# Second pass: the first layer's second product as seven half-size block products, its weights cut by output half

## The chip, the cores and the metric

One core of a Trainium2 chip runs the whole program. TensorE (PE in the profile; PEld is its loading of the stationary operand) does the matmuls, VectorE (DVE) and ScalarE (ACT) the element work, and SyncE (SP) issues nearly all DMAs, in its program's order. The metric is device microseconds of one execution; the median of the runs counts.

## The reference, cut to what matters

```python
x = softmax(30 * tanh(q @ k.T / 8 / 30)) @ v     # 4 batches, 12 heads, 448 positions, head size 64
x = x.transpose(0, 2, 1, 3).reshape(1792, 768)
h = x @ w_in                                     # first layer: 768 -> 2048
x = (h - np.tanh(h)) @ w_out                     # 2048 -> 768
h = x @ w_in2                                    # second layer
out = (h / (1 + np.exp(-1.702 * h))) @ w_out2
```

All weights arrive as 64-bit floats. The rows that count here are the two products with a 2048 x 768 matrix, above all `(h - tanh(h)) @ w_out`.

## The kernel before, in words

**Precision.** Each operand of the four large products is kept as two fp32r tiles, a rounded part and what is left (`xh`/`xl`, `gh`/`gl`, `wh`/`wl`). A product takes three matmuls for each block: high by high, low by high, high by low.

**Stages.** `attention` comes first, in 24 pair steps `g`. Then the 1792 rows go through both layers in two passes of 896 rows (two batches of 448). Each pass runs `gemm_in(0)` (first layer, first product, L648), `gemm_out` (first layer, second product, L667), `gemm_in(1)` (L648 again) and a last product by rows: `gemm_out_rows` (L690) in the first pass, `gemm_rows_seven` (L743, L728) in the second. The 896 columns of `x` and `g` are streamed as 512 and 384 (`SPANS`); the weights are the stationary operand except in the last product.

**Weights.** They come in chunks of the list `chunks`, used in the order of `stream`. In the first pass each chunk is loaded as 64-bit (`dbl_dma`, tile `wd`), converted by six steps on ScalarE and VectorE (`conv_exp` to `conv_lo`, tiles `wr`, `wh`, `wl`), and its two halves are stored to DRAM (`kept`). In the second pass they are loaded back: `w_next` takes the next chunk, `ahead` calls `prepare(i + LEAD)` with `LEAD` 2, so loads run two chunks ahead; the pool `whl` holds three chunks. `gemm_out` uses 18 chunks: six output blocks by three parts of the 2048.

**The last product of the second pass** uses seven block products of half size in place of eight (Strassen-Winograd form). Its weights need sums of blocks, `t1` to `t4`. `weight_combos` makes them: for each of four quarters `j` it loads eight halves (`load_sum`), adds and subtracts on VectorE, splits on ScalarE and VectorE (`keep_split`), and stores eight halves. It is a generator; each call of `ahead` advances it one step (`side`). The left sums of `g` are made beside the matmuls by `left`, into the tiles `ring`.

**What sets the order.** The attention part and `gemm_in` are pinned to the order written. Elsewhere a list scheduler places the instructions of each engine, so the order of the built program is not that of the code: in the built kernel before, most of `weight_combos` stands beside `gemm_in(0)` of the second pass. An engine runs its own list strictly in order, SP too: a DMA that waits for its source holds back all DMAs behind it.

**Early work.** In `attention`, `early` names nine chunks that are loaded and converted there; `conv_at` and `split_at` are tables that say in which pair step. `load_qk`, `load_v` issue the inputs of a step.

Of the kernel before, what the change touches and what calls it, by code (L numbers as in the profile page):

```python
# [29 lines left out]
LATE_AT = 8  # L30
# [7 lines left out]
def attention_moe_moe(ctx, tc, q, k, v, cap, w_in1, w_out1, w_in2, w_out2, out):  # L38
# [82 lines left out]
    parts = [(0, 6), (6, 11), (11, 16)]  # L121
    WG = 3
    chunks = []
    for layer, (wi, wo) in enumerate(((w_in1, w_out1), (w_in2, w_out2))):
        wi, wo = wi.bitcast(U32), wo.bitcast(U32)
        for f in range(KF):
            chunks.append((wi[:, 2 * f * P:2 * (f + 1) * P], 0, KM, P))
        if layer == 0:
            for e in range(KM):
                for f0, f1 in parts:  # L130
                    chunks.append((wo[:, 2 * e * P:2 * (e + 1) * P], f0, f1, P))
        else:
            for half in range(2):
                for f in range(0, KF, 2):
                    chunks.append((wo[:, 2 * half * HW:2 * (half + 1) * HW], f, f + 2, HW))
# [50 lines left out]
    def conv_lo(i):  # L186
        h, l = whl[i]
        n = width[i]
        lo_dve(l[:, :n], raws.pop(i)[:, :n], h[:, :n])
# [5 lines left out]
    def convert(i):  # L195
# [7 lines left out]

    R0 = NCH - KF
    KQ = KF // 4
    combos = {m: [dr_p.tile([P, 2, WC], F32, name=f"{m}_{j}") for j in range(KQ)] for m in ("t1", "t2", "t3", "t4")}
    block = {
        "b11": kept[R0:R0 + KQ],
        "b21": kept[R0 + KQ:R0 + 2 * KQ],
        "b12": kept[R0 + 2 * KQ:R0 + 3 * KQ],  # L210
        "b22": kept[R0 + 3 * KQ:],
        **combos,
    }
    PRODUCTS = ("b11", "t2", "b21", "t3", "t1", "t4", "b22")
    stream = [(kept[i], width[i], chunks[i][3]) for i in range(NCH)] * (NPASS - 1)
    stream += [(kept[i], width[i], chunks[i][3]) for i in range(R0)]
    stream += [(t, WC, HW) for m in PRODUCTS for t in block[m]]

# [45 lines left out]
    def weight_combos():  # L264
        for j in range(KQ):
# [4 lines left out]
            r11, r12, r21, r22 = slots  # L270
            for dst, m in zip(slots, ("b11", "b12", "b21", "b22")):
                load_sum(dst, block[m][j])
                if m != "b22":
                    yield
            t1 = wr_p.tile([P, WC], F32, tag="wr", name="t1")
            hi = wr_p.tile([P, WC], F32, tag="wr", name="t1h")
            nc.vector.tensor_tensor(out=t1, in0=r12, in1=r11, op=ALU.subtract)
            nc.vector.tensor_tensor(out=r12, in0=r22, in1=r12, op=ALU.subtract)
            nc.vector.tensor_tensor(out=r11, in0=r12, in1=r11, op=ALU.add)
# [604 lines left out]
```

## Time and profile before

| | us |
|---|---|
| median of 3 runs (1141.86 to 1146.07) | 1145.31 |
| profiled execution | 1144.08 |
| its span | 1142.3 |

| stage of the profiled execution | from, to (us) |
|---|---|
| attention | 0 to 214 |
| first pass: L648, L667, L648, L690 | 214 to 334, to 450, to 567, to 683 |
| second pass: L648, L667, L648, L743 with L728 | 683 to 799, to 916, to 1032, to 1138 |

TensorE is busy in 1130.9 of 1142.3 us, VectorE in 705.3, ScalarE in 632.1. A busy TensorE row counts pipelined matmuls, whose records overlap, so the time that a matmul adds is read from the spacing, that is from a stretch divided by its count, and not from the mean duration of one. The same holds for back-to-back instructions of VectorE, whose records overlap by some 0.1 us.

### The profile page before, as it was taken

To read this page: it belongs to the slowest core of one execution; us is meant where nothing else is said; L and a number is where in the kernel's file an instruction comes from. 1 tells how busy PE (TensorE), PEld (TensorE's weight loads), DVE (VectorE), ACT (ScalarE), POOL (GpSimd) and SP (SyncE) were. 2 spreads that over 40 slices of the span, in tenths; PEclk is the share of its full clock that TensorE was granted. 3 is DMA by queue.
4 is the path that set the end of the run, shared out by engine and by line. 5 is a ranking of instruction groups with operands and counts; after the bars stand their busy time and mean duration, and the time that the engine had idled before them with its cause. 6 is when DMAs were issued, how large, how long until landed. Compare 5 with 4: busy or idle time off the path is not lost.

```text
span 1142.3 us, 15746 instructions
## 1 busy us (share of the span) xinstructions
PE 1130.9 (99%) x5699; PEld 930.3 (81%) x5699; DVE 705.3 (62%) x1096; ACT 632.1 (55%) x923; POOL 1.8 (0%) x16
## 2 busy tenths in 40 slices
PE   9999999999999999999999999999999999999998
PEld 3443433588888989888999998888898888889998
DVE  4698998699996445777754557999500022445441
ACT  6889998799995444666644427888200022213230
POOL 0000000000000000000000000000000000000000
PEclk9999999999999999999999999999999999999999
DMA  6476776455447666666687888677833333338784
GB/s 162 102 200 187 201 209 190 163 195 192 157 141 267 237 226 218 220 221 221 229 255 256 281 287 307 208 270 268 284 103 106 120 111 111 111 111 282 227 265 153
DMA packets 165022, 230.00 MB, mean 201 GB/s; under 512 B 59680, under 2 KB 112464, under 8 KB 164944
## 3 DMA queue, kind: packets, MB, share of 16 engines
q1 hardware_dynamic: 162496, 227.84, 61.9%
q10 hardware_dynamic: 2448, 1.15, 0.4%
q8 instruction: 45, 0.74, 0.3%
q14 instruction: 33, 0.27, 0.1%
HBM read 157.68 MB, written 71.26 MB: 200 GB/s over the span
## 4 chain that ended last, share of the span: by engine, by line
PE 96%; DMA 3%; DVE 1%; SPq 0%; ACT 0%; issue 0%; DVEq 0%
PE ps_h L648 41%; PE ps_y L667 20%; PE ps_o L690 10%; PE ps_o L743 7%; PE ps_sc L362 5%; PE ps_pv L395 5%; PE ps_sc L358 1%; PE ps_o L728 1%; PE ps_pv L392 1%; PE ps_r L404 1%; PE ps_qk L338 1%; PE ps_qk L347 1%; DMA wd<-in_moe_w_in_dram 1%; DMA wh<-t 0%; DMA raw<-in_k_dram 0%; DMA wl<-t 0%
## 5 line engine op out<-in xcount | busy, mean ns | idle before, releaser
L648 PE MATMUL ps_h<-xh,wh 128*128 128x384 f32 (+1 forms) x768 | 279.2, 364 | 1.7 <-DMA wh<-kept 1.7
L648 PE MATMUL ps_h<-xl,wh 128*128 128x512 f32 (+1 forms) x768 | 280.5, 365 | 0.0
L648 PE MATMUL ps_h<-xh,wl 128*128 128x512 f32 (+1 forms) x768 | 174.7, 362 | 0.0
L648 PEld LDWEIGHTS ps_h<-xh,wh 128*128 128x128 f32 x768 | 144.1, 188 | 18.6 <-DMA wh<-kept 2.4
L648 PEld LDWEIGHTS ps_h<-xl,wh 128*128 128x128 f32 x768 | 144.2, 188 | 16.4
L648 PEld LDWEIGHTS ps_h<-xh,wl 128*128 128x128 f32 x768 | 139.5, 188 | 16.3 <-issue 1.4
L667 PE MATMUL ps_y<-gl,wh 128*128 128x384 f32 (+1 forms) x384 | 140.4, 366 | 0.0
L667 PE MATMUL ps_y<-gh,wh 128*128 128x384 f32 (+1 forms) x384 | 139.7, 364 | 0.0
L667 PE MATMUL ps_y<-gh,wl 128*128 128x384 f32 (+1 forms) x384 | 88.4, 362 | 0.0
L588 ACT ACTIVATE g_t<-ps_h 128x512 f32<-128x512 f32 x64 | 34.9, 546 | 91.4 <-PE ps_h L648 90.6
L82 DVE TENSOR_TENSOR wl<-wr,wh 128x768 fp32r<-128x768 f32 (+1 forms) x66 | 61.4, 931 | 36.7 <-PE ps_y L667 18.9
L160 ACT ACTIVATE wr<-wd 128x768 f32<-128x768 f32 (+1 forms) x66 | 57.8, 877 | 47.0 <-DVE wl L82 32.5
L177 DVE SCALAR_TENSOR_TENSOR wr<-wd,wr 128x768 uint32<-128x768 uint32 (+1 forms) x66 | 61.6, 933 | 30.5 <-ACT wd L165 29.4
L76 ACT CAST wh<-wr 128x768 fp32r<-128x768 f32 (+1 forms) x66 | 53.6, 812 | 46.2 <-PE ps_y L667 29.9
L667 PEld LDWEIGHTS ps_y<-gl,wh 128*128 128x128 f32 x384 | 72.1, 188 | 8.3
L667 PEld LDWEIGHTS ps_y<-gh,wh 128*128 128x128 f32 x384 | 72.0, 188 | 8.1
L667 PEld LDWEIGHTS ps_y<-gh,wl 128*128 128x128 f32 x384 | 69.8, 188 | 7.6
L690 PE MATMUL ps_o<-wh,gh 128*128 128x384 f32 x224 | 74.8, 334 | 0.0
L690 PE MATMUL ps_o<-wl,gh 128*128 128x384 f32 x224 | 74.8, 334 | 0.0
L690 PE MATMUL ps_o<-wh,gl 128*128 128x384 f32 x224 | 74.8, 334 | 0.0
L374 ACT ACTIVATE t<-ps_sc,tsc 128x896 f32<-128x896 f32 x72 | 69.8, 1003 | 6.8 <-PE ps_sc L362 5.9
L82 DVE TENSOR_TENSOR xl<-ps_y,xh 128x512 fp32r<-128x512 f32 (+1 forms) x24 | 14.9, 621 | 93.2 <-ACT xh L76 93.2
(120 smaller groups left out, 1841.1 us busy)
## 6 DMA issues: line engine op xcount, KB each, us to landing
wd<-in_moe_w_in_dram SPq DMA_DIRECT2D x64, 384.0 KB, 4.2
wh<-kept SPq DMA_DIRECT2D x59, 384.0 KB, 3.2
wl<-kept SPq DMA_DIRECT2D x59, 384.0 KB, 4.6
kept<-wh SPq DMA_DIRECT2D x54, 384.0 KB, 3.4
kept<-wl SPq DMA_DIRECT2D x54, 384.0 KB, 3.8
wd<-in_moe_w_out_dram SPq DMA_DIRECT2D x16, 768.0 KB, 5.6
wd<-in_moe_w_out_dram SPq DMA_DIRECT2D x24, 384.0 KB, 4.0
pair<-kept SPq DMA_DIRECT2D x16, 384.0 KB, 6.1
```

The source lines that it names most:

```text
L76: pin(nc.scalar.copy(out=dst, in_=src))
L82: pin(nc.vector.tensor_tensor(out=dst, in0=src, in1=hi.bitcast(F32), op=ALU.subtract))
L160: pin(nc.scalar.mul(out=raws[i][:, :width[i]], in_=dbls[i][:, :, 1].bitcast(F32), mul=2.0 ** -112))
L177: pin(nc.vector.scalar_tensor_tensor(out=u, in0=dbls.pop(i)[:, :, 1], scalar=0x80000007, in1=u, op0=ALU.bitwise_and, op1=ALU.bitwise_or))
L362: pin(nc.tensor.matmul(ps[:, j, :S], qk[a, kc], qk[a, :S], start=True, stop=True))
L374: pin(nc.scalar.activation(out=t, in_=ps, func=AF.Tanh, scale=tsc))
L395: pin(nc.tensor.matmul(ps[j * D:(j + 1) * D, :S], rawv[g][:, j, c, :], tt[g, c][:, j], start=(c == 0), stop=(c == KC - 1)))
L588: nc.scalar.activation(out=t, in_=ps, func=AF.Tanh, scale=0.5 * GELU_C)
L648: pin(nc.tensor.matmul(ps, w[:, kk, :], x[kk][:, a], start=(m == 0), stop=(m == len(seq) - 1)))
L667: nc.tensor.matmul(p[:, :a1 - a0], w[:, f - f0, :], x[f][:, a0:a1], start=(c == 0 and m == 0), stop=(c == len(parts) - 1 and m == len(seq) ...
L690: nc.tensor.matmul(ps[n][:, :HW], g[2 * j + ff][:, a], w[:, ff, :], start=(j == 0 and m == 0), stop=(j == KF // 2 - 1 and m == len(seq) - 1),)
L743: nc.tensor.matmul(ps[n], x[:, t], w[:, kk, :], start=(k == 0 and m == 0), stop=(k == KH - 1 and m == 2),)
```

## The change

1. **Chunks.** The first layer's `w_out` is cut as the second layer's already is: by output half (384 columns) and two blocks of the 2048, 16 chunks of one size in place of 18.
2. **First pass.** `gemm_out` runs over output halves, with six PSUM banks (three output blocks by two spans) open at a time; its results are split by `x_out`.
3. **Second pass.** `gemm_out_seven` takes the place of `gemm_out`: seven products `SEVEN_A`, each 8 blocks of the 2048 by 3 output blocks by 3 matmuls of 448 columns. `right` makes the sums of `g` on VectorE and splits them into `ring`. The partial products are kept in `part` tiles and added on VectorE. So `gemm_in(0)` of this pass leaves `g` unsplit (`gr`).
4. **Weight sums.** `weight_combos(0)` makes `s1` to `s4` from a new single-precision copy (`single`, stored in the first pass by `conv_lo`) beside `gemm_in(0)`; `weight_combos(1)`, that of before, comes one stage later, beside `gemm_out_seven` and `gemm_in(1)`.
5. **Early steps.** The first `load_qk(1)` issues its query half from SP, not from ScalarE; the two first 64-bit loads are issued in steps 1 and 3, not both in step 0; one conversion moves from step 21 to 20, and two splits change places.

```diff
-        if layer == 0:
-            for e in range(KM):
-                for f0, f1 in parts:
-                    chunks.append((wo[:, 2 * e * P:2 * (e + 1) * P], f0, f1, P))
...
+        if A0 <= i < A0 + KF:
+            nc.sync.dma_start(out=single[i - A0], in_=raw_w)
+        if A0 + 2 * KQ <= i < A0 + 3 * KQ:
+            return
...
+    SEVEN_A = ("11", "s2", "12", "s3", "s1", "22", "s4")
...
+                if layer == 0:
+                    nc.sync.dma_start(out=r[m], in_=single[n * KQ + j])
+                else:
+                    load_sum(r[m], block[1][m][j])
...
-    conv_at = [3, 5, 7, 9, 11, 13, 15, 17, 21]
-    split_at = [10, 11, 12, 15, 16, 20, 17, 18, 19, 21, 21, 22]
+    conv_at = [3, 5, 7, 9, 11, 13, 15, 17, 20]
+    split_at = [10, 11, 12, 15, 16, 19, 17, 18, 20, 21, 21, 22]
...
-        load_qk(1, nc.scalar)
+        load_qk(1)
...
-            if g == 0:
-                dbl_dma()
+            if g in (1, 3):
                 dbl_dma()
...
+    def right(p, k):
+        g11, g12, g21, g22 = (gr[f][:, t * S:(t + 1) * S] for f in (k, KH + k) for t in range(2))
+        if p == 1:
+            x = s2[k]
+            nc.vector.tensor_tensor(out=x, in0=g22, in1=g12, op=ALU.subtract)
+            nc.vector.tensor_tensor(out=x, in0=x, in1=g11, op=ALU.add)
+        elif p == 3:
...
+        split(ring[k], x)
...
+    def gemm_out_seven():
...
+        for p, name in enumerate(SEVEN_A):
+            ps = three()
+            for j in range(KQ):
+                i, (wh, wl) = w_next()
+                ahead(i)
+                for kk in range(2):
+                    k = 2 * j + kk
+                    h, l = (t[:, :S] for t in ring[k])
+                    for e in range(3):
+                        c = slice(e * P, (e + 1) * P)
+                        for m, (w, x) in enumerate(((wh, h), (wh, l), (wl, h))):
+                            nc.tensor.matmul(
+                                ps[e], w[:, kk, c], x, start=(k == 0 and m == 0), stop=(k == KH - 1 and m == 2)
+                            )
+                    if p < 6:
+                        right(p + 1, k)
...
+                x_out(3 * m_ + e, slice(s_ * S, (s_ + 1) * S), x)
...
-        yield from gemm_in(0)
-        if last:
-            side.append(weight_combos())
-        gemm_out()
         if last:
             plain[0] = True
             open_plain()
+            side.append(weight_combos(0))
+        yield from gemm_in(0)
+        if last:
+            for _ in side.pop():
+                pass
+            side.append(weight_combos(1))
+        (gemm_out_seven if last else gemm_out)()
         yield from gemm_in(1)
```

Three places of the built order carry terms of the prediction. The first is SP in the second pass, while the first layer's second product runs; a row is one DMA of 128 x 768 words, `wh`/`wl` are weight loads, `pair`/`lo` are loads and `t` stores of `weight_combos`. In the kernel before:

```order
L232 DMA wh_7655<-kept23_196 128x640
L232 DMA wl_7656<-kept23_196 128x640
L232 DMA wh_7699<-kept24_197 128x640
L232 DMA wl_7700<-kept24_197 128x640
L232 DMA wh_7744<-kept25_198 128x768
L232 DMA wl_7745<-kept25_198 128x768
```

In the changed kernel, around the loads of the last product's weights (`s4`):

```order
L257 DMA pair_8178<-kept62_235 128x768
L258 DMA lo_8291<-kept62_235 128x768
L235 DMA wh_8317<-s4_0_261 128x768
L235 DMA wl_8318<-s4_0_261 128x768
L235 DMA wh_8349<-s4_1_262 128x768
L235 DMA wl_8350<-s4_1_262 128x768
L265 DMA t1_2_243<-hi_8322 128x768
L265 DMA t1_2_243<-first_8321 128x768
L235 DMA wh_8391<-s4_2_263 128x768
L235 DMA wl_8392<-s4_2_263 128x768
L265 DMA t3_2_259<-pair_8178 128x768 x2
L235 DMA wh_8417<-s4_3_264 128x768
```

Weight loads that stood alone now have loads and stores of the weight sums between them, and the load of `s4_2` stands behind a store of `first_8321`.

The second place is VectorE at the end of that stage. Before, the last output block's low parts and then the first gate of the next product (`gr`):

```order
L82 TENSOR_TENSOR xl4_124<-ps_y_7958,xh4_118 128x512
L82 TENSOR_TENSOR xl4_124<-ps_y_7959,xh4_118 128x384
L82 TENSOR_TENSOR xl5_125<-ps_y_8085,xh5_119 128x512
L82 TENSOR_TENSOR xl5_125<-ps_y_8086,xh5_119 128x384
L591 SCALAR_TENSOR_TENSOR gr0_8218<-g_t_8317,ps_h_8290 128x512
```

After, from the end of the sixth product (bank `ps_y_8254`):

```order
L729 TENSOR_TENSOR part_7687<-ps_y_8254,part_7687 128x448
L259 TENSOR_TENSOR pair_8178<-pair_8178,lo_8291 128x768
L82 TENSOR_TENSOR xl3_123<-part_7687,xh3_117 128x448
L286 TENSOR_TENSOR pair_8178<-pair_8178 128x768
L263 TENSOR_TENSOR first_8321<-first_8321,hi_8322 128x768
```

and at the end of the seventh:

```order
L729 TENSOR_TENSOR part_7819<-ps_y_8388,part_7819 128x448
L729 TENSOR_TENSOR part_7820<-ps_y_8389,part_7820 128x448
L729 TENSOR_TENSOR part_7821<-ps_y_8390,part_7821 128x448
L82 TENSOR_TENSOR xl0_120<-part_7819,xh0_114 128x448
L82 TENSOR_TENSOR xl1_121<-part_7820,xh1_115 128x448
L82 TENSOR_TENSOR xl2_122<-part_7821,xh2_116 128x448
```

The additions of the weight sums and of the partial products now stand in VectorE's list ahead of what SP and TensorE wait for; the next product starts with `xh0`, `xl0`.

The third place is SP at the end of attention, where the first reload of chunk 0 is issued (`wh<-kept0`). Before:

```order
L413 DMA xd3_3_107<-xs_1967 128x448
L151 DMA wd_1997<-in_moe_w_in_dram 128x3x256 x2
L413 DMA xd3_4_108<-xs_2016 128x448
L232 DMA wh_2049<-kept0_173 128x768
L191 DMA kept14_187<-wh_2025 128x768
```

After:

```order
L446 DMA wb_1985<-wrow1_111 64x448 x2
L145 DMA wd_1966<-in_moe_w_in_dram 128x3x256 x2
L427 DMA xd3_3_107<-xs_2002 128x448
L235 DMA wh_2079<-kept0_173 128x768
L190 DMA kept14_187<-wh_2011 128x768
```

The reload now stands behind the store of step 21's result (`xd3_3`) and no longer behind that of step 22 (`xd3_4`).

## Rows read from the trace of the kernel before

**Rows 1.** The page's part 1: busy us, share of the span, instructions.
```profile
PE 1130.9 (99%) x5699; PEld 930.3 (81%) x5699; DVE 705.3 (62%) x1096; ACT 632.1 (55%) x923; POOL 1.8 (0%) x16
```

**Rows 2.** The chain of waits, second pass's L667 stage: start, us, what.
```profile
799.27 116.40 PE ps_y L667 x576
```

**Rows 3.** Stretches by engine: both L667 stages and the last product.
```profile
core 0: us, PE busy (x) PEld busy (x) DVE busy (x) ACT busy (x) POOL busy (x), PEclk, DMA share, GB/s
799.20:915.60 116.40, 116.40 (x578) 104.42 (x577) 22.15 (x33) 12.56 (x21) 0.00 (x0) 1.00 0.47 151
1031.80:1138.40 106.60, 105.29 (x601) 103.62 (x599) 43.33 (x83) 27.12 (x54) 0.00 (x0) 1.00 0.75 242
333.60:450.10 116.50, 116.50 (x578) 104.52 (x577) 65.05 (x95) 58.83 (x72) 0.00 (x0) 1.00 0.66 227
```

**Rows 4.** The same chain in the two last products by rows (384-column matmuls).
```profile
567.92 115.09 PE ps_o L690 x664
...
1048.58 14.04 PE ps_o L743 x81
...
1080.91 4.65 DMA wl<-t
...
1105.66 5.00 DMA wh<-t
```

**Rows 5.** The chain in attention: eight matmuls of 448 columns.
```profile
36.21 1.70 PE ps_sc L362 x8
```

**Rows 6.** VectorE in order of time, back to back: start, us, instruction.
```profile
200.69 0.62 DVE L79 COPY xs<-ps_pv 128x448 f32<-128x448 f32 x1
201.24 0.62 DVE L474 TENSOR_TENSOR xs<-xs,wb 128x448 f32<-128x448 f32 x1
...
202.36 0.96 DVE L177 SCALAR_TENSOR_TENSOR wr<-wd,wr 128x768 uint32<-128x768 uint32 x1
203.23 0.62 DVE L82 TENSOR_TENSOR xl<-xs,xh 128x448 fp32r<-128x448 f32 x1
```

**Rows 7.** Groups by shape, busy us and mean ns: the cast of 448 columns.
```profile
L76 ACT CAST xh<-x 128x448 fp32r<-128x448 f32 x12 | 6.8, 568 | 23.1 <-DVE x L810 23.1
```

**Rows 8.** DMA issues, reloads of weights: KB each, us to landing.
```profile
wh<-kept SPq DMA_DIRECT2D x59, 384.0 KB, 3.2
wl<-kept SPq DMA_DIRECT2D x59, 384.0 KB, 4.6
```

**Rows 9.** Stretches in which the DMA engines were busiest (second pass's first product).
```profile
690.00:697.00 7.00, 7.00 (x36) 6.25 (x35) 5.83 (x11) 5.48 (x11) 0.00 (x0) 1.00 1.01 375
...
686.00:700.00 14.00, 14.00 (x71) 12.59 (x71) 10.29 (x17) 10.48 (x19) 0.00 (x0) 1.00 0.90 296
...
690.00:704.00 14.00, 14.00 (x71) 12.51 (x70) 12.28 (x21) 11.50 (x22) 0.00 (x0) 1.00 0.96 345
```

**Rows 10.** TensorE in order of time: attention's step 1, and its end.
```profile
25.20 1.72 PE L395 MATMUL ps_pv<-t,rv 128*64 128x448 f32 x8
...
214.29 0.50 PE L648 MATMUL ps_h<-xh,wh 128*128 128x512 f32 x1 [1.67 <-DMA wh<-kept]
```

**Rows 11.** The chain of waits in attention: start, us, what.
```profile
10.98 2.39 DMA raw<-in_k_dram
...
21.64 7.17 DMA wd<-in_moe_w_in_dram
...
34.55 1.65 PE ps_pv L395 x8
...
43.00 1.65 PE ps_pv L395 x8
...
209.75 4.50 DMA wh<-kept
```

**Rows 12.** SP's own issue of two input loads near the start.
```profile
8.34 1.27 SPq L302 DMA_DIRECT2D raw<-in_q_dram  x2
```

**Rows 13.** A stretch in `gemm_in(0)` of the second pass.
```profile
774.00:781.00 7.00, 7.00 (x37) 6.30 (x36) 7.00 (x13) 5.55 (x11) 0.00 (x0) 1.00 0.48 159
```

More of the change, by code (lines that the diff above doesn't have):

```diff
@@ L127, in attention_moe_moe @@
             chunks.append((wi[:, 2 * f * P:2 * (f + 1) * P], 0, KM, P))
-        if layer == 0:
-            for e in range(KM):
-                for f0, f1 in parts:
-                    chunks.append((wo[:, 2 * e * P:2 * (e + 1) * P], f0, f1, P))
[L132 to L135, printed above, removed]
+        for half in range(2):
+            for f in range(0, KF, 2):
+                chunks.append((wo[:, 2 * half * HW:2 * (half + 1) * HW], f, f + 2, HW))
     NCH = len(chunks)
@@ L262, in keep_split, with weight_combos @@
             nc.sync.dma_start(out=dst[:, m], in_=t)
-    def weight_combos():
+    def weight_combos(layer):
+        names = (("11", "12", "21", "22"), ("11", "21", "12", "22"))[layer]
         for j in range(KQ):
@@ new lines, in weight_combos, with op @@
+            first_ = wr_p.tile([P, WC], F32, tag="wr", name="first")
+            hi = wr_p.tile([P, WC], F32, tag="wr", name="hi")
+            def op(out, a, kind, b):
+                nc.vector.tensor_tensor(out=out, in0=a, in1=b, op=kind)
+            if layer == 0:
+                op(first_, r["21"], ALU.add, r["22"])
+                op(r["21"], r["11"], ALU.subtract, r["21"])
+                op(r["11"], first_, ALU.subtract, r["11"])
+                op(r["12"], r["12"], ALU.subtract, r["11"])
+                made = (("s1", first_, hi), ("s3", r["21"], r["22"]), ("s2", r["11"], None), ("s4", r["12"], None))
+            else:
+                op(first_, r["12"], ALU.subtract, r["11"])
+                op(r["12"], r["22"], ALU.subtract, r["12"])
+                op(r["11"], r["12"], ALU.add, r["11"])
+                op(r["21"], r["21"], ALU.subtract, r["11"])
+                made = (("t1", first_, hi), ("t3", r["12"], r["22"]), ("t2", r["11"], None), ("t4", r["21"], None))
@@ L288, in weight_combos @@
+            yield
+            for m, x, h in made:
+                keep_split(block[layer][m][j], x, h or wr_p.tile([P, WC], F32, tag="wr", name="hi"))
                 yield
@@ L572, in rest @@
             nc.vector.copy_predicated(out=q, mask=m.bitcast(U16), data=far)
-            splits.append(g_split(a, f, q))
+            if not plain[0]:
+                splits.append(g_split(a, f, q))
             for _ in last:
                 pass
+            if plain[0] and f < KH and a.stop == NT:
+                right(0, f)
         def rest_behind():
@@ L581, in g_cubic @@
         late.append(rest_behind)
-        if f == KF - 1 and a.stop == NT:
+        if f == KF - 1 and a.stop == NT and not plain[0]:
             late.append(lambda: list(splits.pop(0)))
@@ L636, in left @@
             x = {0: g11, 2: g12, 5: g22}[p]
-        split(ring[k], x)
+        split([t[:, :TH] for t in ring[k]], x)
     def gemm_in(layer):
@@ L673, in gemm_out @@
                             ahead(i)
-                        if m == LATE_AT:
+                        if a0 == 0 and e == 1:
                             run_late()
-            for (a0, a1), p in zip(SPANS, ps):
-                hi_act(xh[e][:, a0:a1], p[:, :a1 - a0])
-                lo_dve(xl[e][:, a0:a1], p[:, :a1 - a0], xh[e][:, a0:a1])
+                    if j == KF // 2 - 1:
+                        for e in range(3):
+                            x_out(3 * half + e, slice(a0, a1), bank[e][:, :a1 - a0])
@@ L821, in moe @@
             open_plain()
+            side.append(weight_combos(0))
[5 more added lines that the diff above has]
+        (gemm_out_seven if last else gemm_out)()
         yield from gemm_in(1)
+        if last:
+            for _ in side.pop():
+                pass
         (gemm_rows_seven if last else gemm_out_rows)(b0)
```

155 lines of the change are left out of this document (100 added, 55 removed).

## The prediction

> **What bounds the kernel now.** The page's first part says TensorE: busy in 1130.9 of 1142.3 us [rows 1]. That alone is weak, since its records overlap, so the next view is the chain of waits stage by stage. In the second pass's first-layer second product the chain is one piece, 576 matmuls in 116.40 us with nothing between them [rows 2]: 0.2021 us each, at a mean of 448 columns (512 and 384 in equal number). No other engine matters there: VectorE is busy 22.15 of 116.40 us and DMA moves 151 GB/s [rows 3]. So a matmul taken out is time taken out, as long as nothing else becomes late. The last product shows where such a form hurts: its matmuls cost 14.04/81 = 0.1733 us, the 588 of them (504 of L743, 84 of L728) are 101.9 us, and the stage takes 106.6 [rows 3, 4], so 4.7 us go into waits, the two longest pieces of them for weight loads.
>
> **The change part by part.** I sum against the profiled execution, 1144.1 us (span 1142.3 and 1.8 outside it).
>
> *Matmuls.* Seven products of 8 x 3 x 3 are 504 matmuls of 448 columns for 576 of the same mean width: 72 less. This form is not in the trace at 448 columns. From below it costs 0.1733 us (384 columns [rows 4]); from above 0.213, eight attention matmuls of 448 columns in 1.70 us [rows 5]. I take 0.2021, since that mixes a narrower and a wider matmul of the same type and the price is in proportion to columns. 504 x 0.2021 = 101.9 us, **-14.5 us**. At 0.213 the gain is 9.0, and 0.1733 would make it 29.1, which I give no weight.
>
> *VectorE in the new stage.* The built order has 141 instructions there: 106 of 448 columns, 32 of 768, 3 of 384. Back to back they follow each other at 0.55 and 0.87 us [rows 6], so 58 + 28 + 1.5 = 88 us beside 102 of TensorE. Each product's sums are made while the product before runs, a lead of up to 14.55 us (72 x 0.2021), so I cost this at nothing. With the recorded durations of 0.62 and 0.96 as prices it is 98 us: still under, but the cover is thin (a rival below).
>
> *The end of the stage.* Before, the next product started without a gap [rows 2]. Now its first matmuls need `xh0`, `xl0`, which come from the seventh product. Bank 0 is ready 6 matmuls early, 1.2 us. Then VectorE adds (0.62), ScalarE casts (0.57 [rows 7]), and `xl0` stands behind the two other additions (the second place above): the last bank's addition starts about 0.2 us after the last matmul and holds VectorE 0.55, then `xl0` takes 0.62 [rows 6]: 1.4 us after the end, when 0.2 would have done. **+1.2 us**, between 1 and 2.5.
>
> *DMA in the new stage.* A weight half is 384 KB [rows 8], 393 KB in thousands. At the best rate of the trace, 375 GB/s with the DMA engines fully busy [rows 9], it takes 1.05 us. In SP's list from the third to the seventh product there are 76 such transfers: 40 weight halves and 36 of `weight_combos(1)`, which used to lie beside the first product and now meets 28 chunks of weights where there were 18 smaller ones. 76 x 1.05 = 79.7 us of transfer for 5 x 14.55 = 72.8 of TensorE: 6.9 too much. A load is issued two chunks ahead, 2 x 18 x 0.2021 = 7.28 us, and lands 3.2 to 4.6 us later [rows 8], so some 3.3 us can be late unseen. **+3.6 us.** The lower bound is 0, if the first two products run ahead enough. The upper one takes the best stretch of 14 us that I found, 345 GB/s [rows 9]: 1.14 us, 86.6, a loss of 10.5.
> The Trainium skill's DMA: Bandwidth & Descriptors (Specifications) states a limit of about 358 GB/s that HBM gives one core. Rows 9 show 375 over 7 us, so the measurement goes above it. By 358 a half would take 1.10 us, the loss would be 7.4 and the sum 1138.4; I stay with the row.
>
> *SP behind VectorE.* In the seventh product the load of `s4_2` stands behind the store of `first_8321`. VectorE makes that after the sixth product's end by an addition, a `load_sum`, an `xl` and two instructions of 768: 0.55 + 0.87 + 0.55 + 0.87 + 0.96 = 3.8 us, less some 0.6 as the bank is early: issue 3.2 us late, landing 0.4 + 4.6 us on, 8.2 for a lead of 7.28. The next load loses 0.6 more in the same way. **+1.5 us**, from 0 to 3. The last product shows the price of such a pattern: the two pieces of rows 4 that wait for a load.
>
> *Attention.* Step 1 to step 2 took 34.55 - 25.20 = 9.35 us against 8.45 in the next one [rows 10, 11]: the two 64-bit loads (7.17 us on the chain) hold up an input. They are now apart: -0.9. At the end TensorE stands 1.67 us for the first reload [rows 10], 4.50 us after its issue [rows 11]; that issue stood behind step 22's store and now stands behind step 21's (the third place), one step of 8.45 us earlier: -1.67. Against it, two query loads join SP's list at the start, 1.27 us of issue [rows 12], ahead of a key load on the chain [rows 11]: +1.27. **-1.3 us**, from -3 to +1.
>
> *At nothing.* The first pass's `gemm_out` keeps its 576 matmuls; its new chunk form is that of L690, where 664 matmuls ran in one piece [rows 4]. The `single` stores add 16 halves and drop 8, 3.1 MB in 116.5 us or 27 GB/s on 227 [rows 3]; the six results per half hide behind the 18 matmuls of the other span. In `gemm_in(0)` of the second pass VectorE was already busy 7.00 of 7.00 us with TensorE at 7.00 [rows 13], and it loses more (32 low parts of `g`) than it gains (8 of `ring`, some early sums). If that cover were gone, one late us would cost one.
>
> Sum: 1144.1 - 14.5 + 1.2 + 3.6 + 1.5 - 1.3 = 1134.6; the median lay 1.2 above the profiled run, which I leave to the range. I forecast **1134.5**, own range 1131 to 1139.
>
> **The rivals.**
> (1) *Nothing waits for DMA*: the loads of the first two products run ahead and the stores come in time. 1144.1 - 14.5 + 1.2 - 1.3 = **1129.5**. For it: bursts of 375 GB/s left TensorE at 7.00 of 7.00 [rows 9]. Against it: there a chunk lasts twice as long.
> (2) *DMA holds the stage at 345 GB/s*: 10.5 for 3.6 us, **1141.5**. For it: 375 GB/s held for 7 us, but not for 14 [rows 9].
> (3) *Slower.* DMA falls to the 296 GB/s of 686 to 700 [rows 9], since loads, stores and reloads of freshly stored sums mix. A half takes 1.33 us, 76 take 101, and every product waits for weights: 101 - 72.8 - 3.3 = 24.9 in place of 3.6 + 1.5, **1154**. The change stops paying where the loss is 14.6: (72.8 + 3.3 + 14.6)/76 = 1.19 us a half, 330 GB/s; it is 0.5% slower below 310. Against it: share was 0.90 there, so the queue was not always full.
> (4) *VectorE becomes the bound.* At 98 us and a wait of 1 us for ScalarE at each of seven turns the stage lasts 105, 3.2 over TensorE: **1138**.
> (5) *The matmul does not get cheaper with its width*: at 0.213 us, 5.5 on top, **1140**.
>
> **How the numbers follow.** Forecast 0.52, (1) 0.20, (2) 0.14, (3) 0.06, (4) 0.05, (5) 0.03. The range 1128 to 1143 leaves out (3) and the tails of (1) and (2). 0.5% of 1145.3, about what a measurement can tell, is 5.7 us: faster is below 1139.6, slower above 1151. Faster: 0.52 + 0.20 + 0.05 and a little of (2) = 0.79; same: the rest of (2), (5) and a tail of the forecast, 0.15; slower: 0.06.
>
> **What would show it.** Profile after: 504 matmuls at about 0.202 us by spacing, the stage near 108 us in place of 116.4; TensorE idle there for weight loads, mostly from the fourth product on and at two chunks of the seventh; 1 to 2 us at the next stage's start; DMA share near 1 in the stage's second half; no wait of 1.67 us at 214; the step 1 to 2 period at 8.45. Wrong it would be if TensorE waits for `ring` (VectorE), if the loss in the stage passes 14 us, or if the first pass's L709 stage leaves 116.5.

## The result and the profile after

The changed kernel takes **1134.53 us** (median of 6, 1132.57 to 1137.46) beside 1144.39 for the kernel before (6 runs): a ratio of 0.9916, 95% interval 0.9896 to 0.9936. The forecast was 1134.5, in a range of 1128 to 1143. So the total was met; its terms were not all met, and misses cancelled.

The profiled execution took 1134.45 us, with a span of 1132.6. The stages, from the first matmul of one to the first matmul of the next in both traces:

| | before, us | after, us |
|---|---|---|
| start to the first pass's second product | 333.70 | 331.35 |
| that product (L667, now L709) | 116.40 | 116.27 |
| the three stages behind it | 349.02 | 349.01 |
| second pass, first layer's second product (L667, now L743) | 116.39 | 108.72 |
| the next product (L648, now L684) | 116.27 | 117.16 |
| the last product, to its last matmul | 106.26 | 105.97 |
| sum | 1138.04 | 1128.46 |

Of the 9.6 us, 7.7 come from the new stage and 2.35 from the first row (attention and the first product); 0.9 goes back at the start of the next product. The page's first part (columns as in [rows 1]) has 72 matmuls less and 73 us more of VectorE:

```profile
PE 1119.7 (99%) x5627; PEld 920.0 (81%) x5627; DVE 778.1 (69%) x1206; ACT 660.5 (58%) x961; POOL 1.8 (0%) x16
```

The chain of waits in the second pass answers to [rows 2]; columns are start, us, what. `s` are the weights of `weight_combos(0)`.

```profile
680.52 116.27 PE ps_h L684 x576
796.78 55.81 PE ps_y L743 x270
...
862.22 6.95 DMA wh<-s
869.30 7.65 PE ps_y L743 x36
877.00 9.97 PE ps_y L743 x45
...
896.60 4.37 DMA wh<-s
901.10 2.79 PE ps_y L743 x12
903.92 1.84 DVE part L729 x3
906.34 116.32 PE ps_h L684 x575
```

One piece of 270 matmuls, then two weight loads on the path, then three additions of the partial products. The first 270 already tell of a miss: 55.81/270 is 0.2067 us, not 0.2021. The stretches show what the DMA engines did (columns as in [rows 3]): the first four products, the last three, and a part of these.

```profile
796.60:856.10 59.50, 59.50 (x290) 54.07 (x289) 53.05 (x88) 26.79 (x47) 0.00 (x0) 1.00 0.90 311
856.10:905.30 49.20, 47.08 (x217) 39.38 (x216) 35.84 (x56) 18.03 (x32) 0.00 (x0) 1.00 0.97 362
870.00:888.00 18.00, 17.95 (x85) 15.43 (x84) 13.84 (x23) 6.51 (x12) 0.00 (x0) 1.00 1.03 406
```

TensorE in order of time at the waits (start, us, instruction, and the idle time before it with what ended it):

```profile
860.46 0.44 PE L743 MATMUL ps_y<-rh,wh 128*128 128x448 f32 x1 [0.44 <-DMA wh<-s]
...
896.92 0.44 PE L743 MATMUL ps_y<-rh,wh 128*128 128x448 f32 x1 [0.62 <-DMA wh<-s]
...
901.10 0.44 PE L743 MATMUL ps_y<-rh,wh 128*128 128x448 f32 x1 [0.22 <-DMA wh<-s]
...
905.34 0.47 PE L684 MATMUL ps_h<-xh,wh 128*128 128x512 f32 x1 [0.25 <-DMA wh<-kept]
906.34 0.50 PE L684 MATMUL ps_h<-xl,wh 128*128 128x512 f32 x1 [0.52 <-DVE xl L82]
```

Every wait is for a weight load, but the last, which is for `xl0`. They are short, and the granted clock stayed at 1.00, the level of 2.4 GHz. The idle times on record in the stage add up to only some 2 us, since records of matmuls overlap; what the waits cost is read from the spacing. SP's own list says how the first came about; behind it stand ScalarE's cast that made `hi`, and the DMA engines meanwhile:

```profile
849.10 0.38 SPq L235 DMA_DIRECT2D wl<-s  x1
854.00 0.32 SPq L265 DMA_DIRECT2D t<-hi  x1
855.67 0.32 SPq L265 DMA_DIRECT2D t<-first  x1
856.08 0.38 SPq L235 DMA_DIRECT2D wh<-s  x1
```

```profile
853.14 0.83 ACT L76 CAST hi<-first 128x768 fp32r<-128x768 f32 x1
```

```profile
851.50:854.00 2.50, 2.50 (x14) 2.27 (x13) 2.13 (x4) 1.31 (x2) 0.00 (x0) 1.00 0.46 183
```

A chunk of weights lasts 18 matmuls, 3.72 us, and its load is due when the chunk two ahead of it begins; so the one at 856.08 was due at 852.4. It stood behind two stores of weight sums that ScalarE (`hi`) and VectorE (`first`) had not made yet, was issued 3.7 us late and landed 4.2 us on, just ahead of the matmul of 860.46. While SP stood there the DMA engines ran short of work: a share of 0.46 from 851.5 to 854.

The other waits can be read in the same way, by how late a load was issued and how long it took to land (the last of its semaphore's updates in the trace); the wait is what the chunk before lasts beyond 3.72 us. The loads for the chunks that begin at 860.46, 864.94, 896.92 and 901.10 were issued 3.1 to 4.1 us late, all behind stores of weight sums, and landed after 4.2 to 5.6 us, which in the first four products nothing had to wait for: 2.5 us of the stage's 4.6 are SP's order. The loads for the three chunks from 873.07 to 880.92 were at most 0.4 us late but took 7.6 to 7.8 us, with the DMA engines full: 0.5 us. One of them:

```profile
873.02 0.32 SPq L235 DMA_DIRECT2D wh<-kept  x1
```

It landed at 880.79, and the matmul at 880.92 waited for it. The remaining 1.6 us fall on loads that were both late (1.5 to 2.4 us) and slow (5.4 to 7.0 us).

Counted by products of 72 matmuls (from the starts of the matmuls; without a wait 72 x 0.2067 = 14.88):

| us | 1 | 2 | 3 | 4 | 5 | 6 | 7 | stage | next product |
|---|---|---|---|---|---|---|---|---|---|
| changed kernel | 14.88 | 14.88 | 14.88 | 14.88 | 16.93 | 15.70 | 16.57 | 108.72 | 117.16 |
| `x3_store_pool` | 14.88 | 20.28 | 14.60 | 14.59 | 18.43 | 14.60 | 16.20 | 113.57 | 121.88 |
| `x5_store_behind` | 14.87 | 14.88 | 16.04 | 15.36 | 14.73 | 16.97 | 14.92 | 107.78 | 117.13 |
| `x2_combos_late` | 14.87 | 14.88 | 14.88 | 14.88 | 14.88 | 14.88 | 15.12 | 104.39 | 126.44 |
| `x8_spread` | 14.87 | 14.88 | 14.88 | 14.88 | 14.88 | 14.88 | 14.88 | 104.15 | 116.30 |
| `x11_496_400` | 14.59 | 14.59 | 14.59 | 14.60 | 14.59 | 14.59 | 14.59 | 102.14 | 116.33 |

### The profile page after: what moved, and what is told of

Read it like the earlier page. It is cut to its first block, busy times and chain, and to the rows that moved or that the text cites. A ratio compares the mean times of both kernels' runs of the same rounds, so it can differ in the third digit from the quotient of the medians.

```text
span 1132.6 us, 15911 instructions
## 1 busy us (share of the span) xinstructions
PE 1119.7 (99%) x5627; PEld 920.0 (81%) x5627; DVE 778.1 (69%) x1206; ACT 660.5 (58%) x961; POOL 1.8 (0%) x16
## 4 chain that ended last, share of the span: by engine, by line
PE 93%; DVE 3%; DMA 2%; ACT 2%; issue 0%; SPq 0%; DVEq 0%; ACTq 0%
PE ps_h L684 41%; PE ps_o L793 10%; PE ps_y L709 10%; PE ps_o L846 7%; PE ps_y L743 7%; PE ps_sc L376 5%; PE ps_pv L409 5%; PE ps_o L831 1%; PE ps_pv L406 1%; PE ps_sc L372 1%; PE ps_r L418 1%; PE ps_qk L352 1%; DMA wh<-s 1%; PE ps_qk L361 1%; ACT t L388 1%; DVE pair L286 0%
## 5 line engine op out<-in xcount | busy, mean ns | idle before, releaser
L684 PE MATMUL ps_h<-xl,wh 128*128 128x512 f32 (+1 forms) x768 | 280.6, 365 | 0.5 <-DVE xl L82 0.5
L684 PE MATMUL ps_h<-xh,wh 128*128 128x384 f32 (+1 forms) x768 | 279.4, 364 | 0.3 <-DMA wh<-kept 0.3
L684 PE MATMUL ps_h<-xh,wl 128*128 128x512 f32 (+1 forms) x768 | 174.7, 362 | 0.0
L684 PEld LDWEIGHTS ps_h<-xl,wh 128*128 128x128 f32 x768 | 144.2, 188 | 17.5 <-DVE xl L82 0.8
L684 PEld LDWEIGHTS ps_h<-xh,wh 128*128 128x128 f32 x768 | 144.1, 188 | 16.9 <-ACT xh L76 0.6
L684 PEld LDWEIGHTS ps_h<-xh,wl 128*128 128x128 f32 x768 | 139.5, 188 | 16.3 <-issue 1.4
L154 ACT ACTIVATE wr<-wd 128x768 f32<-128x768 f32 x64 | 57.5, 900 | 49.3 <-DVE wl L82 25.3
L82 DVE TENSOR_TENSOR wl<-wr,wh 128x768 fp32r<-128x768 f32 x64 | 61.2, 956 | 31.6 <-ACT wh L76 26.3
L171 DVE SCALAR_TENSOR_TENSOR wr<-wd,wr 128x768 uint32<-128x768 uint32 x64 | 61.3, 958 | 29.4 <-ACT wd L159 28.4
L76 ACT CAST wh<-wr 128x768 fp32r<-128x768 f32 x64 | 53.4, 834 | 46.5 <-PE ps_y L709 24.3
L82 DVE TENSOR_TENSOR rl<-gr,rh 128x448 fp32r<-128x448 f32 (+1 forms) x80 | 46.9, 589 | 42.5 <-ACT rh L76 42.4
L390 ACT ACTIVATE t<-t,cpos 128x896 f32<-128x896 f32 x72 | 72.0, 1036 | 0.0
L709 PE MATMUL ps_y<-gl,wh 128*128 128x512 f32 (+1 forms) x192 | 69.8, 364 | 0.0
L709 PE MATMUL ps_y<-gh,wh 128*128 128x512 f32 (+1 forms) x192 | 69.7, 363 | 0.0
L376 PE MATMUL ps_sc<-qk 64*128 64x448 f32 x288 | 67.1, 571 | 0.0
L409 PE MATMUL ps_pv<-t,rv 128*64 128x448 f32 x288 | 64.8, 556 | 1.2 <-ACT t L390 0.8
```

The costliest lines, as they stand in the source:

```text
L76: pin(nc.scalar.copy(out=dst, in_=src))
L82: pin(nc.vector.tensor_tensor(out=dst, in0=src, in1=hi.bitcast(F32), op=ALU.subtract))
L171: pin(nc.vector.scalar_tensor_tensor(out=u, in0=dbls.pop(i)[:, :, 1], scalar=0x80000007, in1=u, op0=ALU.bitwise_and, op1=ALU.bitwise_or))
L376: pin(nc.tensor.matmul(ps[:, j, :S], qk[a, kc], qk[a, :S], start=True, stop=True))
L390: ins = pin(nc.scalar.activation(out=tt[g, c], in_=tt[g, c], func=AF.Exp, scale=cpos))
L409: pin(nc.tensor.matmul(ps[j * D:(j + 1) * D, :S], rawv[g][:, j, c, :], tt[g, c][:, j], start=(c == 0), stop=(c == KC - 1)))
```

## The experiments

### What a matmul of 448 columns costs

```diff
+        spans = (((0, 448), (448, NT)), ((0, 464), (464, NT)), ((0, 496), (496, NT)), SPANS)[n_in[0]]
...
-            for a0, a1 in SPANS:
+            for a0, a1 in spans:
...
-                for (a0, a1), bank in zip(SPANS, ps):
+                for (a0, a1), bank in zip(((0, 480), (480, NT)), ps):
```

> The changed kernel, with the 896 columns cut elsewhere: first pass 448+448 in the first product, 480+416 in the second, 464+432 in the third; second pass 496+400 in the first product; the rest as it is. Question: why a matmul of the seven products took 0.2067 us where 0.2021 had been forecast. Theory A, the price is that of the width 448, whatever the stage: the first stage shows 0.2067 at both of its spans and lasts 119.1 us in place of 116.3 (576 x 0.2067). Theory B, the price comes from the form of the stage (weights by three output blocks, banks changed after three matmuls): 448 columns cost 0.2019 there and the stage lasts 116.3. For the other widths a straight line between 384 (0.1748) and 512 (0.2290) gives 0.1816, 0.1883, 0.1951, 0.2086, 0.2154, 0.2222 at 400, 416, 432, 464, 480, 496, and stages of 116.3; under A they may lie above it, each stage up to 3 us longer. Whole kernel 1137 by A with 448 alone dear, 1145 if all six widths are, 1134.5 by B.

1135.08 us in one execution. In the first pass's first product the 576 matmuls of 448 columns came every 0.2067 us, apart from two waits at its start that the changed kernel has too (the stage is 2.6 us longer): theory A. The other widths lie within 2 ns of the straight line: 0.1833, 0.1868, 0.1937, 0.2099, 0.2172, 0.2202 at 400, 416, 432, 464, 480, 496. So 448 alone is dear. But the same kernel's seven products began at 0.2027, the first four without a break. TensorE in order of time, 8 spacings of the first product, then 7 of the seven products:

```profile
299.73 0.37 PE L688 MATMUL ps_h<-xl,wh 128*128 128x448 f32 x1
...
301.38 0.37 PE L688 MATMUL ps_h<-xl,wh 128*128 128x448 f32 x1
...
799.71 0.36 PE L747 MATMUL ps_y<-rl,wh 128*128 128x448 f32 x1
...
801.13 0.36 PE L747 MATMUL ps_y<-rh,wl 128*128 128x448 f32 x1
```

1.65/8 = 0.206 and 1.42/7 = 0.203, at a granted clock of 1.00 in both. There are two rhythms, each kept for whole products where nothing waits; the last two runs take this up. At a wait the rhythm can change, either way: in the changed kernel too, about half of the 216 matmuls of the last three products came at 0.2027, which took 0.4 us off 5.0 us of waits.

### Where the waits of the seven products come from

First with the sums for the last product taken out of the stage:

```diff
+        for _ in range(per[0] if side else 0):
...
+                    behind.enter_context(tc.issue_after(load[0].ins))
...
+        (gemm_out_seven if last else gemm_out)()
+        if last:
             side.append(weight_combos(1))
-        (gemm_out_seven if last else gemm_out)()
+            per[0] = 3
```

> The changed kernel with the weight sums for the last product (weight_combos(1)) taken out of the seven-product stage and made beside the product after it, three steps per chunk, each queued on SP behind the chunk's weight load. Theory: all 4.6 us that TensorE waited in that stage beyond 504 x 0.2067 come from these sums (their transfers, and their stores ahead of weight loads in SP's list): the stage lasts 104.2 to 104.6 us, 4.2 to 4.6 less, and the kernel about 1130; the next stage keeps its 116.3, as its chunks last twice as long. Rival, the stage's own 56 weight halves and VectorE's sums make the waits: it stays near 108.7 and the kernel at 1134.5. Rival, the sums are only moved: 4 us come back as waits of the next stage or the last product, 1134 again.

1135.78 us (ratio 0.994, 0.992 to 0.9959). The stage did as the theory said: 104.39 us, so the waits do come from these sums. But the next product took 126.44: the third case held, and more than was gained came back. The chain there, and the clock behind the wait:

```profile
902.46 60.95 PE ps_h L690 x299
963.41 6.38 DMA wh<-kept
```

```profile
970.00:980.00 10.00, 10.00 (x41) 8.61 (x42) 7.07 (x11) 2.83 (x5) 0.00 (x0) 0.83 0.70 264
```

SP was stuck ahead of a load of the sums from 958.7 to 963.0, and TensorE stood 2.58 us; a second wait, for VectorE, was 3.4 us. After each, matmuls of 512 columns came every 0.43 us for some 3 us, against 0.23: the lower of the two clocks (1.2 GHz), some 1.4 us more each. That the sums hurt more where chunks last twice as long was not in my reckoning. They are not quite the same bytes: all 64 transfers of the sums lie in this stage here, while the changed kernel has 42 of them in the seven products, 8 ahead and 14 behind. Three steps per chunk is a burst, and each of these two waits cost its length and the slow matmuls behind it.

Then two ways to keep the bytes in the stage and take the stores from in front of the weight loads. First another queue:

```diff
-            nc.sync.dma_start(out=dst[:, m], in_=t)
+            q.dma_start(out=dst[:, m], in_=t)
...
+                keep_split(block[layer][m][j], x, h or wr_p.tile([P, WC], F32, tag="wr", name="hi"), nc.gpsimd if layer else nc.sync)
```

> The changed kernel with the stores of weight_combos(1) issued from GpSimd in place of SP: the same bytes in the same stage, but no weight load stands behind a store that waits for VectorE. Theory S, the order on SP made the waits of the fifth and seventh product (2.05 and 1.69 us beyond 14.88): those two go, the sixth product's 0.8 us stays, the stage lasts 105 to 105.5 and the kernel about 1131. Theory D, the DMA engines were full (0.98 to 1.03 of their time): the waits stay at 4 to 5 us, wherever they show, and the kernel at 1134 to 1135. GpSimd's own issue may take longer, which would make it slower than either.

1143.96 us, ratio 1.0009 (0.9993 to 1.0026): all of the gain gone, by neither theory. The chain in the second product:

```profile
809.84 0.53 POOL t L265
810.37 6.82 DMA t<-pair
...
817.26 0.32 SPq L257
...
817.67 6.33 DMA wh<-s
824.00 0.14 issue
824.14 6.95 PE ps_y L743 x25
```

The store from GpSimd landed 6.82 us after its issue. (The median of the stores of this tile is 6.0 us, and 5.7 from SP in the changed kernel, so the queue by itself is hardly slower.) Until then its buffer was taken, SP's next load into that buffer waited, and the weight load behind it on SP was late. So a store needs not stand in SP's list to hold it; it is enough that a load there wants its buffer. Behind the wait for this weight load, 3.6 us, the granted clock fell as well, to 0.57 from 824 to 828.

Then the same queue, each pair of stores one step later:

```diff
+                if plain[0] and A0 + 4 <= i - NCH < 3 * KF:
+                    behind.enter_context(tc.issue_after(load[0].ins))
+                next(side[0], None)
...
+        if late_stores:
+            yield
         for m, t in enumerate((hi, x)):
             nc.sync.dma_start(out=dst[:, m], in_=t)
```

(`load` is the chunk's weight load; a step of the sums is queued behind it)

> The changed kernel with each pair of stores of weight_combos(1) held back by one step, and so queued on SP behind the weight load of the next chunk: the same bytes from the same queue in the same stage, but a weight load no longer stands behind a store that VectorE still has to make. Theory S, that order made the waits: the fifth and seventh of the seven products fall from 16.93 and 16.57 us to 14.9 to 15.5, the stage from 108.7 to 105 to 106, the kernel to about 1131.5. Theory D, the DMA engines are full there: a wait in the same size, 3.5 to 4.6 us, stays in the stage, perhaps in other products, and the kernel stays at 1134 to 1135.

1132.38 us (ratio 0.9913, 0.9884 to 0.9943). The fifth and seventh product fell to 14.73 and 14.92, as S had it; but 3.6 us of waits stayed in the stage, in the third, fourth and sixth, as D had it. TensorE there, the loads that it waited for in SP's list, and the DMA engines around both:

```profile
840.50 0.44 PE L752 MATMUL ps_y<-rh,wh 128*128 128x448 f32 x1 [1.06 <-ACT rh L76]
...
875.93 0.44 PE L752 MATMUL ps_y<-rh,wh 128*128 128x448 f32 x1 [1.45 <-DMA wh<-kept]
```

```profile
832.19 0.57 SPq L237 DMA_DIRECT2D wh<-s  x1
...
868.58 0.50 SPq L237 DMA_DIRECT2D wh<-kept  x1
```

```profile
836.00:846.00 10.00, 8.94 (x43) 7.68 (x43) 7.98 (x13) 4.05 (x8) 0.00 (x0) 1.00 1.03 406
...
867.00:877.00 10.00, 8.50 (x41) 7.12 (x40) 7.82 (x15) 4.34 (x8) 0.00 (x0) 1.00 1.03 414
```

The profile names `rh` for the first wait, but that cast ended at 840.49, when the weights of this matmul were already going into TensorE (from 840.47); the load of `wh` landed at 840.37. It had been issued 0.3 us late and took 8.2 us, more than the 7.44 that two chunks last: full engines. The load for the second wait was issued 1.7 us late, as SP had stood that long ahead of a load of the sums, and took 7.2: both. So SP's order made more than half of the waits in the changed kernel, as read above; with the stores out of the way the same bytes met full engines earlier, and 3.6 us stayed. Curing the order alone gained 0.9 us in the stage; the sums have to be thinner as well.

### The start of the next product

```diff
-            for a0, a1 in SPANS:
+            for a0, a1 in ((0, 384), (384, NT)) if layer and plain[0] else SPANS:
```

> The changed kernel with the product after the seven cut as 384+512 columns in place of 512+384, so that its first 18 matmuls (3.1 us) need only what the third and the sixth of the seven products gave. Theory: the second matmul of that stage waited 1.00 us (0.23 without a wait) for xl0, which the seventh product gives, and that wait goes: 0.8 us less from the stage's start, kernel about 1133.7. Rival: the wait only moves to the second span, or TensorE then waits for the first weight load (0.25 us before that matmul already) or for VectorE's gates in another order: no change, 1134.5, or 1 us slower.

1133.57 us (ratio 0.9918, 0.989 to 0.9947). TensorE at the same place:

```profile
905.50 0.44 PE L684 MATMUL ps_h<-xh,wh 128*128 128x384 f32 x1 [0.33 <-DMA wh<-kept]
905.79 0.34 PE L684 MATMUL ps_h<-xl,wh 128*128 128x384 f32 x1
```

The second matmul follows after 0.29 us, where it was 1.00, and the product takes 116.36 for 117.16: 0.8 us, as the theory had it. The times alone could not tell a difference so small; the traces do.

### The early steps

```diff
-        load_qk(1)
+        load_qk(1, nc.scalar)
```

> The changed kernel with the two first query loads of step 1 issued by ScalarE again, as before the change. By the prediction's step they cost 1.27 us on SP, ahead of a key load on the chain: without them the first gated matmul comes 1.27 us earlier and the kernel is 1.3 us faster. Rival: with the two 64-bit loads apart nothing at the start waits for SP any more (the chain of the changed kernel has no transfer in its first 45 us), so nothing is gained, and the start can lose what ScalarE then does later: within 0.4 us of 1134.5.

1133.85 us (ratio 0.9919, 0.9901 to 0.9937). Step by step the start comes 0.58 us earlier than in the changed kernel (eight value matmuls at 33.72 and 34.30). Single executions differ: over the eight traces with the query loads on SP the same matmuls of step 1 come at 25.58 to 26.53, 25.85 on average, over the six with them on ScalarE at 25.07 to 25.71, 25.29. So the two query loads on SP cost about half of the 1.27 us forecast: neither the one theory nor the other.

```diff
-            if g in (1, 3):
+            if g == 0:
+                dbl_dma()
                 dbl_dma()
...
-    conv_at = [3, 5, 7, 9, 11, 13, 15, 17, 20]
+    conv_at = [3, 5, 7, 9, 11, 13, 15, 17, 21]
```

(with the two splits and the query loads put back as well)

> The changed kernel with all early steps put back as before the change (both 64-bit loads in step 0, the conversion of step 20 in step 21, the two splits in their old steps, the first query loads from ScalarE). By the prediction attention gets 1.3 us longer: +0.9 for the period from step 1 to step 2, +1.67 for the first reload at the end, -1.27 for the query loads. By the two traces 2.1 us: 0.25 at the start, 1.67 at the end, the rest in the stall at 187 to 198. The first product would be entered 1.3 to 2.1 us later, the kernel at 1135.8 to 1136.6. Rival: the end is set by something else (the chunks of the first pass were cut anew as well): within 0.4 of 1134.5.

1136.83 us (ratio 0.995, 0.9935 to 0.9965): 2.3 more than the changed kernel. The first pass's second product began 2.6 later than in the changed kernel's trace above, which alone would show little: a second execution of the changed kernel (the next run) was as late, for another reason. At the start (chain of waits) it was no worse, and at the end of attention (TensorE in order of time) the wait of [rows 10] was back:

```profile
25.17 1.65 PE ps_pv L409 x8
...
34.00 1.65 PE ps_pv L409 x8
```

```profile
213.04 0.50 PE L685 MATMUL ps_h<-xh,wh 128*128 128x512 f32 x1 [2.12 <-DMA wh<-kept]
```

The period from step 1 to 2 is 8.83 us here, and 8.44 with the loads apart. For the kernel before, the 9.35 of the prediction takes its two ends from two views; read in one, TensorE in order of time, it is 34.48 - 25.20 = 9.28. The late reload is the term that counts, the more as the granted clock fell behind it (0.90 on average from 209 to 216).

### The parts alone, and a version built on the findings

> The changed kernel as it is, beside the two other kernels of this comparison: 1132.5 to 1137.5, median near 1134.5, the seven products 108.7 to 109.9 us with the waits in the fifth to the seventh. Whether the seven products' matmuls come at 0.2067 or at 0.2027 us (the width of 448 showed both) is open: 2.0 us in the stage.

1134.15 us (ratio 0.9908, 0.9891 to 0.9924), the seven products 108.64. Its profiled execution, at 1137.19, shows where single times differ: attention's stall near 195, which in most traces here lasts 0.25 to 2.21 us, was 2.68 us long in it, with the clock at the lower level behind it (mean 0.73 in the first row, 0.84 in the next):

```profile
192.00:200.00 8.00, 5.32 (x17) 1.99 (x17) 6.01 (x10) 4.95 (x7) 0.00 (x0) 0.73 0.68 213
200.00:208.00 8.00, 8.00 (x30) 2.51 (x28) 4.84 (x7) 6.95 (x9) 0.00 (x0) 0.84 0.44 138
```

So stages are compared from their own starts here, and a difference in attention between two single traces says little: this one and the first trace of the same kernel enter the first product 2.6 us apart (214.29 and 211.71).

```diff
-        (gemm_out_seven if last else gemm_out)()
+        gemm_out()
```

(eight products in both passes, no single copies, no `weight_combos(0)`, `weight_combos(1)` where it was; the chunks and the early steps of the change stay)

> The changed kernel without the seven products: chunks by output half, the new gemm_out in both passes, the early steps of the change, but eight products in the second pass and weight_combos(1) where it was before the change (no single copies, no weight_combos(0)). By the prediction the chunk form costs nothing, so its first-pass stage and its second-pass stage both take 116.3 and the kernel is before less attention alone: 1144.4 - 2.2 = 1142.2 (by the prediction's own term, 1143.1). The seven products with all that hangs on them are then worth 7 to 8 us. Rival, the chunk form carries part of the gain or a loss: over 1 us off 1142.2, in the stages of the two gemm_out.

1142.09 us (ratio 0.9985, 0.9971 to 0.9998), and both `gemm_out` stages take 116.27. The chunk form costs nothing. What is left of the change there, the early steps, gains 1.7 us on the kernel before (interval 0.2 to 3.3), and the seven products with all that hangs on them are worth 1142.09 - 1134.15 = 7.9 us.

```diff
-            next(side[0], None)
...
+                    behind.enter_context(tc.issue_after(load[0].ins))
+                for _ in range(1 if i < NCH + A0 else (i - NCH) % 2 if i < NCH + A0 + 28 else 2):
+                    next(side[0], None)
```

(`load` is the chunk's weight load; with the later stores, the 384+512 spans and the query loads of the runs above)

> Three edits at once on the changed kernel: weight_combos(1) spread over the seven products (one step in every second chunk) and the product after it (two steps per chunk), its stores one step later and behind the next weight load; the product after the seven cut as 384+512; the first query loads from ScalarE. Traffic is then some 290 GB/s in the seven products and 260 in the next stage, both under the 372 to 406 that the DMA engines moved when full. Theory, the waits come from full DMA engines and add up: 4.3 from the seven products, 0.9 from the next stage's start, 0.6 from the start of attention, so 1134.5 - 5.8 = 1128.7, and the granted clock stays 1.0 throughout. Rival, as where all of the sums lay beside the product after the seven: a wait of 2 us or more remains there, the clock falls after it, and the kernel comes to 1133 or more.

**1127.77 us**, ratio 0.9855 (0.984 to 0.9869), 6.4 less than the changed kernel beside it. The seven products and the next stage:

```profile
795.30:899.50 104.20, 104.20 (x507) 94.66 (x506) 73.88 (x122) 40.11 (x71) 0.00 (x0) 1.00 0.87 303
899.50:1015.80 116.30, 116.30 (x578) 104.38 (x577) 69.20 (x117) 34.19 (x67) 0.00 (x0) 1.00 0.75 252
```

No wait is left in either. With the same sums, 24 of their 64 transfers in the first of these stages and 40 in the second, queued behind the weight loads, all 4.6 us are back: from the third product on the loads of the seven products were issued at most 0.2 us late and landed after 3.1 to 6.0. This run cures the order and the rate together.

Last, the two rhythms, on top of this kernel:

```diff
-            for a0, a1 in ((0, 384), (384, NT)) if layer and plain[0] else SPANS:
+            for a0, a1 in ((0, 384), (384, NT)) if layer and plain[0] else ((0, 496), (496, NT)) if plain[0] else SPANS:
```

> The kernel with the sums spread over two stages (1127.8), and the product before the seven, in the second pass, cut as 496+400 in place of 512+384. Question: what decides between the two rhythms that a matmul of 448 columns showed, 0.2067 and 0.2027 us. Theory, what ran before: the one kernel whose seven products began at 0.2027 had 496+400 just ahead. Then all 504 come at 0.2027, the seven products take 102.2 us in place of 104.15, the stage ahead stays at 116.2, and the kernel is 2.0 us faster, 1125.8. Rival, chance at each start: 0.2067 again in all runs or in some, 1127.8 or a mixture, with single times 2 us apart.

> The same with 464+432 ahead of the seven products. If any cut other than 512+384 brings the shorter rhythm, 1125.8 as well; if 496+400 alone does, or if it is chance, 1127.8 or a mixture. The stage ahead itself takes 116.2 either way (464 and 432 columns showed 0.2099 and 0.1937).

With 496+400 ahead all 504 matmuls came at 0.2027 in the profiled execution, the stage took 102.14, and the kernel **1125.78 us** (ratio 0.9844, 0.982 to 0.9868), the best of this study. With 464+432 they came at 0.2067 in the profiled execution, 104.16, and the kernel took 1128.34. The intervals of `x11_496_400` and `x8_spread` overlap; the traces show the 2 us in the stage. So what ran before seems to decide: two starts behind 496+400, one behind 464+432, nine behind 512+384, and behind each cut the traces show one rhythm alone. That is not proof: one of the four executions with 464+432 took 1125.47, which has no trace and looks like the shorter rhythm, so chance, the rival, is not ruled out. Why there are two rhythms stays open.

## Why the prediction was right, term by term

**Matmuls: -14.5 forecast, -12.2 found.** This is the step that failed. 504 x 0.2067 = 104.2 for 116.4. "I take 0.2021, since ... the price is in proportion to columns" holds for the six other widths measured, but not for 448, 4.6 ns dearer than taken in one rhythm and 0.6 in the other, both inside the bounds (0.1733 and 0.213). The Trainium skill's TensorE: Matmul & The Clock Gate (Back-to-back issue gap) gives, for an isolated matmul at the higher clock, a gap that grows in a straight line with the columns, N/2.4 ns and 2.5 more. By such a line 448 columns lie midway between 384 and 512, as I took it. The rows at 384 and 512 (0.1748 and 0.2290) agree with its slope (0.42 ns a column), not with its constant; the 0.2067 at 448 lies off the line.

**Transfers and SP: +3.6 and +1.5 forecast, +4.6 found.** The sum was right, and so was the cause in the large: without the sums in the stage the waits go (`x2_combos_late`), spread thin and behind the weight loads they go as well (`x8_spread`). The cut into two terms was the wrong way round. Late issue on SP behind stores of weight sums made 2.5 us, full engines 0.5, and 1.6 had both. The waits began with the fifth product, not the fourth, since the pattern forecast for the seventh, a load behind a store that is not made yet, stood in the fifth too; in the seventh it cost 1.2 us. The transfer term rests on a rate that the stage did not keep: 375 GB/s was taken as the best, 406 came over 18 us with the engines full, and 414 over 10 in `x5_store_behind`. At 406 the 76 transfers take 73.6 us, and the term would be nothing; from 826.4 to 905.3 the mean was 354, at a share of 0.95. So the total of the two terms came near in part by luck. The Trainium skill's DMA: Bandwidth & Descriptors (Specifications) states about 358 GB/s; the rows above exceed it, and the loss of 7.4 us estimated from it was not seen. The Trainium skill's Perfetto Trace Analysis (Roofline) sets the ceiling of a core whose neighbour is idle by its 16 engines, about 435 GB/s, and no stretch shown here is above that.

**End of the stage: +1.2 forecast, 0.9 found** (117.16 for 116.27), for the reason given: `xl0` behind VectorE's additions. `x6_spans384` takes it away.

**Attention: -1.3 forecast, -2.35 found**, in single traces that differ by themselves by as much; by the medians of `x9_chunks_only`, -1.7. The reload's wait is confirmed: no wait is left at the start of the first product, and 2.12 us come back when the step is undone. The two start terms were both too large: 0.6 in place of 1.27 for the query loads, and 0.4 in place of 0.9 for the 64-bit loads apart (8.83 against 8.44). The 0.9 came from one execution.

**VectorE: 0 forecast.** It was busy 88.9 of 108.7 us in the stage (53.05 + 35.84 in the rows above), as reckoned (88), and no idle time of TensorE there is put down to `ring`. **The first pass's second product: 0 forecast**, 116.27 found, 0.1 less.

The terms found add up: -12.2 + 4.6 + 0.9 - 2.35 - 0.1 and 0.3 less in the last product are -9.5, the forecast sum was -9.5. The gain in matmuls was 2.3 us too high, and attention and the smaller waits gave that back: the total was right in part by luck. Of the rivals, (1) fell, as TensorE did wait; (2) and (3) fell, as the waits in the stage were 4.6 us where they wanted 12.0 and 24.9; (4) fell; (5), by which the width did not pay, was half true and had been given 0.03.

## What to carry to other kernels

Measure the price of a matmul at its own width before counting on it; a straight line through two other widths missed by 2%, a sixth of the gain. When a change moves side work to another stage, look first for loads that stand behind stores or behind buffers not yet free, add up that stage's transfers against what the DMA engines carry when full, and spread the steps: here the same sums cost 4.6 us with 42 of their 64 transfers in one stage, 10 with all of them in the next, and nothing spread over both. To tell late issue from full engines, read for each load when it was due, when it was issued and how long it took to land. The waits under 1 us cost their length; the two longest in `x2_combos_late` cost some 1.4 us more each, through the clock.

## What was not expected of the hardware

A matmul of 448 columns (fp32r, its weights loaded each time) showed two rhythms at a granted clock of 1.00, 0.2067 and 0.2027 us, kept over hundreds of matmuls. Both starts behind 496+400 had the shorter one; behind 512+384 and 464+432 the traces show the longer, until a wait switched it, as in the changed kernel itself. The DMA engines of one core moved 406 GB/s for 18 us with loads, stores and reloads mixed. A wait's length alone did not tell whether the clock fell. Behind waits of up to 1.45 us in the seven products of `x5_store_behind` the granted clock stayed at 1.00, and so it did behind one of 2.04 us in attention of the changed kernel (195.31) and one of 2.55 us in `x3_store_pool` (869.27); behind those of 2.58 and 3.4 us in `x2_combos_late`, and of 2.12 us in `x7_early_undone`, it fell. What decides between them no run here shows.
